# Decoding double-precision weights by way of PSUM in a fused attention and feed-forward kernel

## The chip, the cores and the metric

One core of a Trainium2 chip runs the kernel. The engines are TensorE (PE; its weight loads are listed apart as PEld), VectorE (DVE), ScalarE (ACT), GpSimd (POOL) and the queues that issue transfers (SP here). SBUF is the working memory, PSUM the memory of eight banks into which TensorE writes. The metric is the device time in microseconds of one execution; the median of several runs counts.

## What is computed

Attention over 4 batches, 8 heads, 768 rows and a head size of 64, with a window of 96 rows, 8 global columns and a linear bias; then a feed-forward network (FFN) on the 3072 rows, whose activation is a ratio of two polynomials:

```python
def reference(q, k, v, n_global, n_local, w_in, w_out, a, b):
    scores = q @ k.T / 8 - slope * dist          # kept: local window or global columns
    x = softmax(scores) @ v                      # rows x 512
    h = x @ w_in                                 # 512 -> 2048
    P = a[0] + a[1] * h + a[2] * h**2 + a[3] * h**3
    Q = 1 + abs(b[0]) * abs(h) + abs(b[1]) * h**2
    return (P / (Q + 1e-6)) @ w_out              # 2048 -> 512
```

The weights `w_in` and `w_out` (named `moe_w_in` and `moe_w_out`) arrive as 64-bit floats. [...]

## The kernel before

The rows are worked through in 12 chunks of 256. Attention runs in 96 units (`t` counts them), each a block of 128 rows and two heads; the FFN runs in 96 steps (`f`), eight for each chunk, each with 256 of the 2048 inner columns. Step `f` starts 10 units behind attention at first. In one pass of the loop over `t` stand one attention unit, one FFN step, and for the first 17 units two or four weight pieces to decode (`WSCHED`). A scheduler reorders all of it by the priorities `PRI_A` and `PRI`, and each engine then works through its own list strictly in order.

Names: `tk` are the transposed q and k of a unit, `s` its scores, `pr` its probabilities, `tp` and `pT` these transposed, `o` its output, `x` (later `xh` and `xl`) the FFN's input. `h` is the first product of an FFN step, `fu`, `fa`, `fs` and `q` its activation, `acc` the second product. The first chunk multiplies plain 32-bit weights (`w_..f`, L274 and L353). For the later chunks each weight is split into a high part (`w_..h`, L233) and a low part (`win_l`, `wout_l`, L234), each product made of three (L282 and L358).

A weight piece is 128 rows by 512 columns; there are 32, 16 for each matrix. A transfer of 512 KB brings its words (`r_..`) into one of five buffers, `fetch` starts it. `decode` then makes the piece of the upper word `top` and the lower word `low`: the magnitude of the upper word, scaled by 2^-112 (so that its exponent fits); the top bits of the lower word as an integer (`half` scaled and rounded); sign and that integer joined (L218); and the magnitude shifted by three bits and joined with it (L220). Which engine scales is set for each piece by the table `MODE`: in mode 5 GpSimd scales the magnitude (L211, nine pieces), else ScalarE (L213); `half` is scaled by GpSimd (L215) but for the first piece (L217). Everything of this lies in SBUF. A buffer comes free for the next transfer with the last operation.

PSUM's eight banks are shared out by pools: `ps_h` two (tag h), `ps_o` two (acc), `ps_r` one (tag r, the tile q of the activation), `ps_t` three (tag t: tk, s, tp and o in turn).

Of the kernel before, what the change touches and what calls it, by code (L numbers as in the profile page):

```python
# [9 lines left out]
F32 = mybir.dt.float32  # L10
FR = mybir.dt.float32r
I32 = mybir.dt.int32
BF16 = mybir.dt.bfloat16
U16 = mybir.dt.uint16
AF = mybir.ActivationFunctionType
ALU = mybir.AluOpType
PSUM = bass.MemoryType.PSUM

P = 128
# [3 lines left out]
FLOOR = -0.5 + 2.0 ** -14  # L23
# [16 lines left out]

SPLITS = {4: 0, 5: 2, 6: 4, 7: 8, 8: 12, 9: 16, 10: 19, 11: 22, 12: 25, 13: 28, 14: 32}

MODE = (3, 5, 2, 5, 2, 5, 2, 5, 2, 5, 2, 5, 2, 2, 5, 2, 2, 5, 2, 2, 5, 2, 2, 2, 2, 2, 2, 2, 2, 2, 2, 2)
HI_V = (0, 2, 4, 6, 8, 10, 12, 14, 16, 18, 20, 22, 24, 26, 28, 30)
LO_V = (13, 15, 17, 19, 21, 23, 25, 27, 29, 31)

# [59 lines left out]
def tile_kernel(ctx: ExitStack, tc: tile.TileContext, q, k, v, n_global, n_local,  # L106
                w_in, w_out, ca, cb, out):
    nc = tc.nc
# [5 lines left out]
    TOK = 2 * P  # L114
# [8 lines left out]
    pl = SimpleNamespace(tmps=TMPS, gbufs=GBUFS, split=False)  # L123
# [34 lines left out]
    full = {}  # L158
    hi = {}

    def piece(dt, key):
        return wide.tile([P, 2 * TOK], dt, tag="w", name=f"w{'_'.join(map(str, key))}{'f' if dt is F32 else 'h'}",
                         bufs=NCT * DF // (2 * TOK) + NFT + 1)
# [11 lines left out]
    def fetch(key, eng=nc.sync):  # L175
        z, r, j = (*key, 0)[0:3]
        r = slice(r * P, (r + 1) * P)
        src = w_in_i[r, 4 * j * TOK:4 * (j + 1) * TOK] if z else w_out_i[r, :]
        home = (pl.early, "raw", 2) if (len(full) + len(fetched)) % 5 in (1, 3) else (pl.ffn, "g", pl.gbufs)
        raw = home[0].tile([P, 2, 2, TOK], F32, tag=home[1], name="r" + "_".join(map(str, key)), bufs=home[2])  # L180
        raw = fetched[key] = raw.rearrange("p z a b -> p (z a b)").rearrange("p (f w) -> p f w", w=2)
        eng.dma_start(out=raw.bitcast(I32), in_=src.rearrange("p (f w) -> p f w", w=2))

    def decode(key):
        dst = full[key] = piece(F32, key)
        if key not in fetched:
            fetch(key)
        raw = fetched.pop(key)
        bits = dst.bitcast(I32)
        top, low = raw.bitcast(I32)[:, :, 1], raw.bitcast(I32)[:, :, 0]  # L190
        half = raw.bitcast(U16).rearrange("p f (w z) -> p f w z", z=2)[:, :, 0, 1]
        mode = MODE[len(full) - 1]
        if mode < 2:


            nc.scalar.activation(out=dst, in_=raw[:, :, 1], func=AF.Abs)
            guard = nc.gpsimd if mode else nc.vector
            guard.tensor_scalar(out=dst, in0=dst, scalar1=1.125 * 2.0 ** -15, scalar2=None, op0=ALU.max)
            nc.vector.tensor_scalar(out=bits, in0=bits, scalar1=3, scalar2=0x3FFFFFFF,
                                    op0=ALU.logical_shift_left, op1=ALU.bitwise_and)  # L200
            nc.vector.scalar_tensor_tensor(out=bits, in0=top, scalar=-0x40000000, in1=bits,
                                           op0=ALU.bitwise_and, op1=ALU.bitwise_or)
            nc.vector.scalar_tensor_tensor(out=bits, in0=low, scalar=29, in1=bits,
                                           op0=ALU.logical_shift_right, op1=ALU.bitwise_or)
            return

        if mode == 5:  # L210
            nc.gpsimd.tensor_scalar(out=dst, in0=raw[:, :, 1], scalar1=2.0 ** -112, scalar2=None, op0=ALU.mult)  # L211
        else:
            nc.scalar.activation(out=dst, in_=raw[:, :, 1], func=AF.Abs, scale=2.0 ** -112)  # L213
        if mode != 3:
            nc.gpsimd.tensor_scalar(out=low, in0=half, scalar1=2.0 ** -13, scalar2=FLOOR, op0=ALU.mult, op1=ALU.add)  # L215
        else:
            nc.scalar.activation(out=low, in_=half, func=AF.Copy, scale=2.0 ** -13, bias=FLOOR)  # L217
        nc.vector.scalar_tensor_tensor(out=low, in0=top, scalar=-0x80000000, in1=low,  # L218
                                       op0=ALU.bitwise_and, op1=ALU.bitwise_or)
        nc.vector.scalar_tensor_tensor(out=bits, in0=bits, scalar=3, in1=low,  # L220
                                       op0=ALU.logical_shift_left, op1=ALU.bitwise_or)

    w_in_i = w_in.bitcast(I32)
    w_out_i = w_out.bitcast(I32)
# [333 lines left out]
    def windowed(lates):  # L558
# [33 lines left out]
        for t in range(NU + LAG + F2 + 1):  # L592
# [75 lines left out]
            for n, (kind, j) in enumerate(WSCHED.get(t, ())):  # L668
                tc.cur_priority = base + 1000 * t + pri[False]["dec"] + 50 * n
                for key in pieces(kind, j):  # L670
                    decode(key)
# [162 lines left out]
```

## Time and profile before

| | |
|---|---|
| median of 3 runs | 760.51 us (758.7 to 760.87) |
| the profiled execution | 762.41 us, its span 760.6 us |
| busy in the span | PE 730.6, PEld 635.3, DVE 609.0, ACT 577.6, POOL 455.4 us |
| mean granted clock of TensorE | 0.993 |
| weights decoded | between 8.8 and 100.6 us |
| DVE idle | none between 60 and 97.5 us |
| PE in the chain that ended last | 87% |

The span is cut by what each engine does. Busy time of PE is modelled from its pipelined matmuls, so a PE that waits briefly between two of them still shows as busy; how much it really worked is read from the number of its records and from what one takes where nothing waits. A wait is put down to the event that ended it. Everything that the change touches lies in the first 105 us of the span.

### The profile page before, as it was taken

How to read it: one execution, taken by the hardware profiler on the slowest of the kernel's cores; microseconds unless marked ns; L12 is line 12 of the kernel's file. 1: busy time of each engine (PE TensorE's matmuls, PEld its weight loads, DVE VectorE, ACT ScalarE, POOL GpSimd, SP SyncE). 2: the span in 40 equal slices, each digit the busy share in tenths (PEclk: the TensorE clock that was granted, in tenths of full speed). 3: DMA queues.
4: the chain of work that ended last, by engine and by line, in shares of the span. 5: the costliest groups of instructions: out<-in, count | busy, mean ns of one | idle time of the engine just before them, and what ended most of it. 6: DMA issues, size and time to landing. Idle time of an engine off the chain costs nothing.

```text
span 760.6 us, 15061 instructions
## 1 busy us (share of the span) xinstructions
PE 730.6 (96%) x5072; PEld 635.3 (84%) x5072; DVE 609.0 (80%) x1440; ACT 577.6 (76%) x1302; POOL 455.4 (60%) x488
## 2 busy tenths in 40 slices
PE   4788989999999999999999999999999999999996
PEld 3566657788988988998999989988988988998995
DVE  5789985888798878888788878778888788886565
ACT  5687866986887877877877877877887878776764
POOL 4585665584666666746656656566466656665441
PEclk9999999999999999999999999999999999999999
DMA  8876500204332322323322322233322331200000
GB/s 232 254 245 181 185 22 15 57 22 111 91 79 69 104 64 58 101 64 74 101 53 58 101 61 66 84 78 77 89 59 64 90 72 37 71 16 1 28 1 33
DMA packets 111959, 62.17 MB, mean 82 GB/s; under 512 B 81664, under 2 KB 100096, under 8 KB 111872
## 3 DMA queue, kind: packets, MB, share of 16 engines
q1 hardware_dynamic: 111584, 61.11, 29.8%
q8 instruction: 42, 0.69, 0.4%
q14 instruction: 45, 0.37, 0.2%
q10 hardware_dynamic: 288, 0.00, 0.0%
HBM read 35.92 MB, written 6.29 MB: 55 GB/s over the span
## 4 chain that ended last, share of the span: by engine, by line
PE 87%; DVE 6%; DMA 2%; issue 2%; POOL 1%; ACT 1%; SPq 0%; DVEq 0%; POOLq 0%
PE h L282 34%; PE acc L358 33%; PE o L522 5%; PE tp L497 5%; PE s L449 4%; PE acc L353 3%; DVE r L218 2%; DMA r<-in_moe_w_in_dram 2%; PE s L444 1%; PE tk L394 1%; PE h L274 1%; DMA nat<-in_k_dram 1%; DVE pr L463 1%; PE o L513 0%; POOL r L215 0%
## 5 line engine op out<-in xcount | busy, mean ns | idle before, releaser
L487 POOL TENSOR_SCALAR pr<-pr,stats 128x256 f32<-128x256 f32 (+1 forms) x152 | 132.9, 885 | 108.8 <-DVE stats L478 64.5
L282 PE MATMUL h<-xh,win_l 128*128 128x256 f32 x704 | 197.5, 281 | 0.0
L315 POOL TENSOR_TENSOR fa<-fa,fs 128x512 f32<-128x512 f32 x95 | 125.1, 1317 | 83.2 <-ACT fs L308 73.2
L358 PE MATMUL acc<-wout_l,g 128*128 128x512 f32 x352 | 139.4, 396 | 0.0
L282 PEld LDWEIGHTS h<-xh,win_l 128*128 128x128 f32 x704 | 133.1, 189 | 2.0 <-issue 0.5
L338 POOL TENSOR_TENSOR g<-fu,g 128x512 fp32r<-128x512 f32 x87 | 113.9, 1309 | 32.0 <-ACT g L337 25.9
L473 ACT ACTIVATE pr<-pr,stats 128x256 f32<-128x256 f32 (+1 forms) x192 | 92.7, 485 | 30.8 <-DVE stats L463 28.9
L306 ACT ACTIVATE fu<-h,coef 128x512 f32<-128x512 f32 (+1 forms) x97 | 75.1, 774 | 27.8 <-PE h L282 23.9
L327 DVE SCALAR_TENSOR_TENSOR fu<-fu,coef,q 128x512 f32<-128x512 f32 (+1 forms) x97 | 71.7, 739 | 29.9 <-ACT q L323 27.3
L322 ACT ACTIVATE fs<-fa,coef 128x512 f32<-128x512 f32 (+1 forms) x97 | 69.5, 716 | 27.6 <-POOL fa L315 25.8
L313 DVE TENSOR_TENSOR fu<-fu,h 128x512 f32<-128x512 f32 (+1 forms) x97 | 65.5, 675 | 16.8 <-ACT fs L308 16.7
L358 PEld LDWEIGHTS acc<-wout_l,g 128*128 128x128 f32 x352 | 66.4, 189 | 9.6
L314 DVE SCALAR_TENSOR_TENSOR fu<-fu,coef,h 128x512 f32<-128x512 f32 (+1 forms) x97 | 71.7, 739 | 1.9
L427 DVE SCALAR_TENSOR_TENSOR kq<-tk,kq 64x256 fp32r<-64x256 f32 x144 | 60.8, 422 | 14.7 <-ACT kq L426 10.5
L328 DVE SCALAR_TENSOR_TENSOR q<-fa,coef,q 128x512 f32<-128x512 f32 (+1 forms) x97 | 72.1, 743 | 0.0
L499 DVE COPY pT<-tp 128x512 f32<-128x512 f32 (+1 forms) x75 | 48.4, 645 | 28.0 <-PE tp L497 26.9
L426 ACT ACTIVATE kq<-tk 64x256 fp32r<-64x256 f32 x144 | 54.3, 377 | 19.2 <-DVE kq L427 13.5
L308 ACT ACTIVATE fs<-h,coef 128x512 f32<-128x512 f32 (+1 forms) x97 | 66.3, 684 | 2.0 <-DMA out_dram<-o 1.8
L329 DVE SCALAR_TENSOR_TENSOR fu<-q,fu 128x512 f32<-128x512 f32 (+1 forms) x97 | 66.1, 681 | 1.6
L337 ACT CAST g<-fu 128x512 fp32r<-128x512 f32 (+1 forms) x89 | 54.8, 615 | 15.0 <-DVE fu L329 14.6
L307 ACT ACTIVATE fa<-h,coef 128x512 f32<-128x512 f32 (+1 forms) x97 | 65.6, 676 | 0.0
L497 PE MATMUL tp<-ident,pr 128*128 128x128 f32 x352 | 57.3, 275 | 2.5 <-DVE stats L463 2.4
(253 smaller groups left out, 2049.0 us busy)
## 6 DMA issues: line engine op xcount, KB each, us to landing
mv<-nat SPq DMA_DIRECT2D x36, 256.0 KB
qT<-kq SPq DMA_DIRECT2D x144, 64.0 KB
r<-in_moe_w_in_dram SPq DMA_DIRECT2D x16, 512.0 KB
r<-in_moe_w_out_dram SPq DMA_DIRECT2D x16, 512.0 KB
nat<-in_q_dram SPq DMA_DIRECT2D x48, 128.0 KB
nat<-in_k_dram SPq DMA_DIRECT2D x48, 128.0 KB
vt<-in_v_dram SPq DMA_DIRECT2D x48, 128.0 KB
out_dram<-o SPq DMA_DIRECT2D x24, 256.0 KB
```

The costliest lines, as they stand in the source:

```text
L282: nc.tensor.matmul(out=hps[f][:, y, :], lhsT=w[:, fs], rhs=x[:, ct, :], start=(n == 0), stop=(n == 3 * NCT - 1))
L306: nc.scalar.activation(out=u, in_=h, func=AF.Identity, scale=a3, bias=a2)
L314: nc.vector.scalar_tensor_tensor(out=u, in0=u, scalar=a1, in1=h, op0=ALU.add, op1=ALU.mult)
L315: side(f).tensor_tensor(out=a, in0=a, in1=s, op=ALU.add)
L322: nc.scalar.activation(out=s, in_=a, func=AF.Ln, bias=q1)
L327: nc.vector.scalar_tensor_tensor(out=u, in0=u, scalar=a0, in1=r, op0=ALU.add, op1=ALU.mult)
L328: nc.vector.scalar_tensor_tensor(out=r, in0=a, scalar=q1, in1=r, op0=ALU.add, op1=ALU.mult)
L338: side(f).tensor_tensor(out=g[:, 1, ys], in0=u, in1=g[:, 0, ys], op=ALU.subtract)
L358: nc.tensor.matmul(out=acc, lhsT=gs[f][:, z, y, ts], rhs=w, start=(ft == 0 and n == 0), stop=(ft == NFT - 1 and n == 2))
L473: nc.scalar.activation(out=d, in_=d, func=AF.Exp, scale=-1.0, bias=st[:, x:x + 1], accum_out=st[:, 2 + 2 * x:3 + 2 * x])
L487: nc.gpsimd.tensor_scalar(out=d, in0=d, scalar1=st[:, 6 + x:7 + x], scalar2=None, op0=ALU.mult)
L497: nc.tensor.transpose(out=t_ps[:, x, w, :], in_=pr[:, x, w, :], identity=ident)
```

## The change

The magnitude is no longer made in SBUF: every piece has a tile `mag` in PSUM (name `m`), which ScalarE writes for all 32 pieces. DVE's first operation shifts it and joins it with the scaled lower word, in place in PSUM; the second adds the sign from the upper word and writes the piece to SBUF. GpSimd scales the lower words only, as before (31 of 32). The first 16 pieces take their tile from the pools of h and r, in turn h, r, h; from the 17th on (`IDLE`) they take it from `ps_t`, the attention tiles' pool. No pool gets larger. The branch for modes 0 and 1, which the table did not use, goes too. All lines behind move up by 13.

```diff
-MODE = (3, 5, 2, 5, 2, 5, 2, 5, 2, 5, 2, 5, 2, 2, 5, 2, 2, 5, 2, 2, 5, 2, 2, 2, 2, 2, 2, 2, 2, 2, 2, 2)
+LOW_A = (0,)
+IDLE = 16
...
-        bits = dst.bitcast(I32)
+        n = len(full) - 1
         top, low = raw.bitcast(I32)[:, :, 1], raw.bitcast(I32)[:, :, 0]
         half = raw.bitcast(U16).rearrange("p f (w z) -> p f w z", z=2)[:, :, 0, 1]
-        mode = MODE[len(full) - 1]
...
-        if mode == 5:
-            nc.gpsimd.tensor_scalar(out=dst, in0=raw[:, :, 1], scalar1=2.0 ** -112, scalar2=None, op0=ALU.mult)
+        pool, tag = ((pl.ps_h, "h"), (pl.ps_r, "r"), (pl.ps_h, "h"))[n % 3] if n < IDLE else (pl.ps_t, "t")
+        mag = pool.tile([P, 2 * TOK], F32, tag=tag, name=f"m{n}")
+        bits = mag.bitcast(I32)
+        nc.scalar.activation(out=mag, in_=raw[:, :, 1], func=AF.Abs, scale=2.0 ** -112)
+        if n in LOW_A:
+            nc.scalar.activation(out=low, in_=half, func=AF.Copy, scale=2.0 ** -13, bias=FLOOR)
         else:
-            nc.scalar.activation(out=dst, in_=raw[:, :, 1], func=AF.Abs, scale=2.0 ** -112)
-        if mode != 3:
             nc.gpsimd.tensor_scalar(out=low, in0=half, scalar1=2.0 ** -13, scalar2=FLOOR, op0=ALU.mult, op1=ALU.add)
-        else:
-            nc.scalar.activation(out=low, in_=half, func=AF.Copy, scale=2.0 ** -13, bias=FLOOR)
-        nc.vector.scalar_tensor_tensor(out=low, in0=top, scalar=-0x80000000, in1=low,
-                                       op0=ALU.bitwise_and, op1=ALU.bitwise_or)
         nc.vector.scalar_tensor_tensor(out=bits, in0=bits, scalar=3, in1=low,
                                        op0=ALU.logical_shift_left, op1=ALU.bitwise_or)
+        nc.vector.scalar_tensor_tensor(out=dst.bitcast(I32), in0=top, scalar=-0x80000000, in1=bits,
+                                       op0=ALU.bitwise_and, op1=ALU.bitwise_or)
```

In the new program the scaling is L200 (ACT) and L204 (POOL), DVE's two operations are L205 and L207; h is made in L261, acc in L340, the scores in L431.

The scheduler's order changes with it. First place: PE, where the FFN begins (step 0 is h_567 before and h_583 after; s_497 is the score of unit 8, s_572 that of unit 9). Before:

```order
L444 MATMUL s_497<-kF,qz 128x256 x2
L400 MATMUL tk_508<-ident,nat_284 128x128 x2
L274 MATMUL h_567<-x_269,w_0_0f 128x256
L274 MATMUL h_567<-x_269,w_1_0f 128x256
L274 MATMUL h_623<-x_269,w_0_0f 128x256
L274 MATMUL h_623<-x_269,w_1_0f 128x256
L497 MATMUL tp_514<-ident,pr_463 128x128 x4
```

After:

```order
L431 MATMUL s_572<-kF,qz 128x256 x2
L387 MATMUL tk_588<-ident,nat_365 128x128 x2
L509 MATMUL o_535<-pT_533,vt_218 64x128 x2
L509 MATMUL o_535<-pT_533,vt_115 64x128 x2
L484 MATMUL tp_607<-ident,pr_515 128x128 x4
L261 MATMUL h_583<-x_273,w_0_0f 128x256
L261 MATMUL h_583<-x_273,w_1_0f 128x256
```

The early matmuls of steps 0 and 1, which used the first half of x, are gone; the FFN starts one unit later in the list, with x complete. Before, PE goes on with step 0 behind the score of unit 10.

Second place: DVE, where x for the first chunk becomes complete (x_269 before, x_273 after) and the first activation follows. Before:

```order
L218 SCALAR_TENSOR_TENSOR r_2_2_484<-r_2_2_484 128x512
L220 SCALAR_TENSOR_TENSOR w_3_2f<-w_3_2f,r_3_2_491 128x512
L220 SCALAR_TENSOR_TENSOR w_2_2f<-w_2_2f,r_2_2_484 128x512
L544 TENSOR_TENSOR x_269<-x_269,o_521 128x2x128
L463 ISA pr_616,stats<-s_612,masks 128x256
```

After:

```order
L207 SCALAR_TENSOR_TENSOR w_2_2f<-r_2_2_496,m_498 128x512
L531 TENSOR_TENSOR x_273<-x_273,o_535 128x2x128
L463 TENSOR_REDUCE stats<-stats 128x2
L465 RECIPROCAL stats<-stats 128x2
L205 SCALAR_TENSOR_TENSOR m_506<-m_506,r_3_2_504 128x512
L207 SCALAR_TENSOR_TENSOR w_3_2f<-r_3_2_504,m_506 128x512
L205 SCALAR_TENSOR_TENSOR m_554<-m_554,r_0_2_552 128x512
L207 SCALAR_TENSOR_TENSOR w_0_2f<-r_0_2_552,m_554 128x512
L205 SCALAR_TENSOR_TENSOR m_562<-m_562,r_1_2_560 128x512
```

The piece w_3_2f stands behind x now. m_554 (the 15th piece) is the last but one magnitude in a bank of h, so step 0's h_583 can have that bank only behind L207 for w_0_2f, four decode operations after x.

Third place: DVE in the stretch where magnitudes lie in the attention tiles' banks. After:

```order
L205 SCALAR_TENSOR_TENSOR m_1040<-m_1040,r_12_1038 128x512
L316 SCALAR_TENSOR_TENSOR fu_1093<-q_1160,fu_1093 128x512
L465 RECIPROCAL stats<-stats 128x2
L205 SCALAR_TENSOR_TENSOR m_1048<-m_1048,r_13_1046 128x512
L207 SCALAR_TENSOR_TENSOR w_12f<-r_12_1038,m_1040 128x512
L207 SCALAR_TENSOR_TENSOR w_13f<-r_13_1046,m_1048 128x512
```

Two magnitudes are held at once, two of the three banks of `ps_t`; L316 of step 6 (fu_1093) stands ahead of the pieces of w_out for that step. Before, w_12f was decoded ahead of the activation of step 3:

```order
L218 SCALAR_TENSOR_TENSOR r_11_932<-r_11_932 128x512
L220 SCALAR_TENSOR_TENSOR w_10f<-w_10f,r_10_925 128x512
L314 SCALAR_TENSOR_TENSOR fu_811<-fu_811,coef,h_793 128x512
L233 CAST w_2_0h<-w_2_0f 128x512
L220 SCALAR_TENSOR_TENSOR w_12f<-w_12f,r_12_1010 128x512
L218 SCALAR_TENSOR_TENSOR r_13_1017<-r_13_1017 128x512
```

So decoding is spread over more FFN steps, the activations of all eight steps of the first chunk now stand ahead of the last decoded piece on DVE (of five steps before, the fifth in part), and the splitting of weights follows behind it.

More of the change, by code (lines that the diff above doesn't have):

```diff
@@ L188, in decode @@
         raw = fetched.pop(key)
-        bits = dst.bitcast(I32)
+        n = len(full) - 1
         top, low = raw.bitcast(I32)[:, :, 1], raw.bitcast(I32)[:, :, 0]
         half = raw.bitcast(U16).rearrange("p f (w z) -> p f w z", z=2)[:, :, 0, 1]
-        mode = MODE[len(full) - 1]
[L193 to L201, printed above, removed]
-                                           op0=ALU.bitwise_and, op1=ALU.bitwise_or)
-            nc.vector.scalar_tensor_tensor(out=bits, in0=low, scalar=29, in1=bits,
-                                           op0=ALU.logical_shift_right, op1=ALU.bitwise_or)
-            return
@@ L215, in decode @@
+        if n in LOW_A:
+            nc.scalar.activation(out=low, in_=half, func=AF.Copy, scale=2.0 ** -13, bias=FLOOR)
+        else:
             nc.gpsimd.tensor_scalar(out=low, in0=half, scalar1=2.0 ** -13, scalar2=FLOOR, op0=ALU.mult, op1=ALU.add)
-        else:
-            nc.scalar.activation(out=low, in_=half, func=AF.Copy, scale=2.0 ** -13, bias=FLOOR)
-        nc.vector.scalar_tensor_tensor(out=low, in0=top, scalar=-0x80000000, in1=low,
-                                       op0=ALU.bitwise_and, op1=ALU.bitwise_or)
```

## The prediction

> **What bounds the kernel now.** I read the chain of waits first, to see which engine sets the end, and from when on.
>
> ```profile
> PE 87%; DVE 6%; DMA 2%; issue 2%; POOL 1%; ACT 1%; SPq 0%; DVEq 0%; POOLq 0%
> ...
> 96.85 0.61 DVE fu L329
> ...
> 97.51 5.40 PE acc L353 x8
> ...
> 103.34 3.46 PE h L274 x16
> 106.80 0.86 PE s L444 x4
> ...
> 119.29 0.47 PE o L513 x5
> ...
> 119.87 0.87 PE o L522 x15
> 120.74 5.35 PE acc L353 x12
> 126.09 0.44 PE tp L497 x4
> ...
> 130.94 0.22 PE tk L400 x2
> ...
> 743.31 10.50 PE acc L358 x44
> ```
>
> TensorE (PE) is 87% of the chain. From 97.5 us to the last matmul at 753.8 the chain holds nothing but PE: there the time is the sum of its work, which the change leaves alone. So only PE's idle time before 97.5 us can be won or lost, apart from new waits behind it. The rows in the middle also price PE's work when it is not waiting: L274 takes 3.46/16 = 216 ns a record, L353 446, L444 215, L497 and L400 110, L513 94, L522 58. Right behind its wait L353 took 5.40/8 = 675 ns, so the eight lost (675 - 446) x 8 = 1.8 us more, at a lower granted clock (below).
>
> Next, the busy time of each engine by stretch (columns: PE, PE's weight loads, DVE = VectorE, ACT = ScalarE, POOL = GpSimd, then granted clock, DMA share, GB/s).
>
> ```profile
> 20.00:30.00 10.00, 7.04 (x39) 4.73 (x38) 6.88 (x23) 6.59 (x27) 3.19 (x5) 0.83 0.89 269
> 30.00:47.20 17.20, 13.42 (x101) 10.13 (x101) 15.35 (x43) 12.99 (x41) 14.19 (x16) 1.00 0.78 245
> 47.20:60.00 12.80, 10.58 (x67) 8.68 (x68) 11.24 (x23) 10.11 (x25) 11.98 (x12) 1.00 0.78 249
> 60.00:97.50 37.50, 33.11 (x170) 23.10 (x168) 37.50 (x71) 28.43 (x65) 21.29 (x22) 1.00 0.54 165
> 97.50:130.00 32.50, 32.49 (x146) 21.64 (x147) 23.82 (x59) 21.07 (x50) 19.92 (x20) 0.95 0.06 13
> ```
>
> From 60 to 97.5 us DVE has no idle moment, and from 30 to 60 POOL is busy 26.2 of 30 us. These are the two engines that the change relieves. The DMA engines are at 0.54 to 0.89: no bound by themselves.
>
> I cut at 47.2 us, where PE takes up the FFN matmuls for good (stage A before, stage B from there to 97.5). PE's busy time counts waiting inside a matmul, so I take records from the trace, in stage B, for L274, L353, L444, L497, L522, L400 and L513 in this order:
>
> ```profile
> 47.20:97.50 50.30, 20.43 (x88) 16.21 (x88) 1.00 0.60 187
> 47.20:97.50 50.30, 11.00 (x24) 4.32 (x24) 1.00 0.60 187
> 47.20:97.50 50.30, 5.34 (x20) 3.56 (x20) 1.00 0.60 187
> 47.20:97.50 50.30, 3.06 (x20) 2.39 (x20) 1.00 0.60 187
> 47.20:97.50 50.30, 3.57 (x48) 2.68 (x48) 1.00 0.60 187
> 47.20:97.50 50.30, 2.29 (x12) 1.70 (x12) 1.00 0.60 187
> 47.20:97.50 50.30, 2.19 (x24) 1.23 (x24) 1.00 0.60 187
> ```
>
> Times the prices above: 88 x 0.216 + 24 x 0.446 + 20 x 0.215 + 20 x 0.110 + 48 x 0.058 + 12 x 0.110 + 24 x 0.094 = 42.6 us of work in 50.3. PE truly idles only 7.7 us in stage B, and with the 1.8 us behind it 9.5 us. That is all that stage B can give back, however much faster decoding gets.
>
> **The change, part by part.** First DVE: the same 64 decode operations, but each reads one input from PSUM.
>
> ```profile
> L218 DVE SCALAR_TENSOR_TENSOR r<-r x32: 674/693/1753, 10.8 to 96.2; 128x512 int32<-128x512 int32 x32
> 0.00:47.20 47.20, 10.42 (x14) 0.96 0.83 246
> 47.20:97.50 50.30, 16.11 (x18) 1.00 0.60 187
> 0.00:47.20 47.20, 10.91 (x14) 0.96 0.83 246
> 47.20:97.50 50.30, 15.53 (x17) 1.00 0.60 187
> L313 DVE TENSOR_TENSOR fu<-fu,h 128x512 f32<-128x512 f32 x6 | 4.0, 675 | 0.0
> L314 DVE SCALAR_TENSOR_TENSOR fu<-fu,coef,h 128x512 f32<-128x512 f32 x6 | 4.4, 734 | 0.0
> L329 DVE SCALAR_TENSOR_TENSOR fu<-q,fu 128x512 f32<-128x512 f32 x5 | 3.4, 677 | 0.0
> ```
>
> The first row gives shortest, median and longest: 674, 693 and 1753 ns, so some run 2.6 times as long as others of one shape. The next four are L218 and L220 by stage. At 0.68 us each, stage A's 28 would take 19.0 us and took 21.3: 2.3 us of stretching. Stage B's 35 would take 23.8 and took 31.6: 7.8 us. In the same stretch the operations with one input in PSUM (h, and q in L329) are not stretched at all, 675 to 734 ns on average; L314 has a per-partition scalar, which the decode has not. I read the stretching as GpSimd standing in the way of operations with two SBUF inputs, and price the new ones at 0.68 us, like L329, which has a constant scalar and one PSUM input: DVE gains 2.3 us in A and 7.8 in B. Bounds: 0.67 (L313) to 0.73 (L314), which would take back 64 x 0.05 = 3.2 us of the 10.1.
>
> [...]
>
> Second, GpSimd loses its nine scalings (L211), and ScalarE takes them.
>
> ```profile
> sum 130.00, POOL 15.47; mean POOL 5.16
> L213 ACT ACTIVATE w_2f<-r x4: 654/664/688, 39.1 to 48.6; 128x512 f32<-128x512 f32 x4
> L323 ACT ACTIVATE q<-fs 128x512 f32<-128x512 f32 x6 | 3.6, 604 | 2.6 <-DVE fu L329 2.6
> DVE r L218 <- POOL r L215: 1.5, 3, 0.8
> ```
>
> L211 is 15.5 us of POOL, in the stretch where POOL was nearly full. On the path it is worth what DVE waited for POOL's L215 between 20 and 47 us: 1.5 us. ScalarE gets nine at 0.66 us, 5.9 us, less what writing PSUM saves on all 32 (L323, PSUM out, 0.60): about 4 us in all. It had 50.3 - 38.5 = 11.8 us free in stage B and 4.2 of 17.2 between 30 and 47: I cost it at nothing. If that cover were gone it would be 4 us.
>
> Third, the PSUM banks. Sixteen decodes use the banks of h and q before the FFN needs them, sixteen (from w_4f on) those of the attention tiles. The order shows two consequences.
>
> ```profile
> PE h L274 <- DVE x L544: 0.6, 1, 0.6
> 0.00:47.20 47.20, 1.91 (x9) 1.47 (x9) 0.96 0.83 246
> PE h L274 <- DVE fu L314: 2.2, 1, 2.2
> PE acc L353 <- DVE fu L329: 2.0, 1, 2.0
> L463 DVE CUSTOM_DVE_ANT_0 pr<-s,masks 128x256 f32<-128x256 f32 x24 | 9.1, 414 | 1.1 <-PE s L444 1.1
> ```
>
> (a) Stage A. Before, PE had 1.9 us of L274 done ahead of 47.2 and then waited only for x. Now h gets its bank when w_0_2f is decoded, and DVE has four decode operations between x and that: 4 x 0.68 = 2.7 us later. PE also has one score (0.86 us) less done by then. Against it: x comes 2.3 (stretching) + 1.5 (POOL) + 1.4 (two decode operations that the order put behind x) = 5.2 us sooner. Sum: 5.2 - 2.7 - 1.9 - 0.9 = -0.3 us, so nothing; between -4 and +4, since x also hangs on attention's own round trips.
>
> (b) Stage B. One FFN step with one attention unit is 16 x 0.216 + 8 x 0.446 + 2.4 (4 L444, 4 L497, 2 L400, 4 L513, 8 L522) = 9.4 us of PE. DVE's part of a step is five FFN operations at 0.68 to 0.73, 3.5 us; attention, two score passes at 0.41 and, by estimate, as much again in small operations, 1.7; and 14 decodes over eight steps, 1.75 at 1.36 us, 2.4: 7.6 us, where stretching (7.8 us in the stage) and weight casts had filled it up. So PE becomes the longest engine, with some start-up: waits like the two above for fu, 2.2 and 2.0 us, remain in kind, and decode tiles now hold up to two of three attention banks (the order has two of them in flight). I leave 5 us of the 9.5 as waits, between 2 and 9.5: gain 4.5.
>
> (c) Behind stage B all weight splitting comes later in the order, next to its use; I cost this at nothing to 3 us, taking 0.
>
> Sum: 0 + 4.5 - 0 = 4.5 us. The profiled execution took 762.41 us (span 760.6), 1.9 over the median of 760.51; taken off the median: **756 us**.
>
> **Rivals.**
>
> - *Decoding is the bound and all of it comes back.* For it: DVE without idle in the row 60:97.50. Against it: PE's 42.6 us of work in 50.3. It needs both stages: 9.5 + 2 from A, 749 us.
> - *No change.* Stage A loses what stage B wins (A at -4), or the dearer PSUM price holds (3.2 us of DVE): 758.5 to 762 us.
> - *Slower: the attention banks.* PE works in order. Where a transpose or score waits for a bank that a decode tile holds, every FFN matmul behind it waits too. One tile is held for the ACT write and two DVE operations, 0.66 + 2 x 0.68 = 2.0 us. Eight pairs of decodes come in that stretch; if each pair stops PE 2.0 us, 16 us go against 9.5, so 767 us. It decides from 9.5/8 = 1.2 us a pair. Against it: bank holders come from engines that then have room, and PE has FFN work ahead of most of these.
>
> **How the numbers follow.** I tell no change within 0.3% (2.3 us) of the median. Chances: my forecast 0.48, all of it back 0.13 (faster together 0.61); no change 0.21; slower by the banks 0.18. The forecast's own range is 751 to 758 (gain 2.3 to 9.5). Over all cases 747 to 765 leaves out about 2 in 10: beyond 749 for a better stage A, and most but not all of the bank case.
>
> **What would show it.** L205 and L207 all at 0.67 to 0.73 us, none above 1 us. POOL under 7 of 10 us between 30 and 60. First L261 matmul (FFN) later in PE's order, at 43 to 48 us, and then one stretch without holes. The chain going over to PE alone earlier than 97.5. Wrong if PE waits for m tiles, or for ACT behind POOL, in sum over 9.5 us after the FFN starts, or if x comes no sooner than 46 us.

## The result: slower, 772.57 us, and the profile after

The changed kernel takes 772.57 us in the median of five runs (771.55 to 773.49), the kernel before 760.51 (five runs, 757.45 to 763.45). The ratio is 1.0161, with a 95% interval of 1.0128 to 1.0195: 12 us slower, where 4.5 us faster was forecast. The profiled executions took 771.55 us (span 769.8) and 762.41 us (span 760.6).

First the same stretches of the kernel after, with two later ones, and behind them these two of the kernel before (columns as in the prediction: PE, PEld, DVE, ACT, POOL, granted clock, DMA share, GB/s).

```profile
20.00:30.00 10.00, 7.88 (x43) 5.23 (x40) 5.76 (x23) 6.66 (x25) 2.33 (x5) 1.00 0.84 268
30.00:47.20 17.20, 11.90 (x92) 8.09 (x90) 15.41 (x50) 16.01 (x48) 5.68 (x12) 1.00 0.84 259
47.20:60.00 12.80, 11.42 (x44) 9.60 (x45) 7.49 (x14) 5.20 (x11) 5.79 (x9) 0.74 0.73 255
60.00:97.50 37.50, 37.50 (x180) 25.77 (x179) 30.91 (x64) 28.35 (x62) 12.09 (x16) 1.00 0.45 133
97.50:130.00 32.50, 29.71 (x152) 19.36 (x150) 22.10 (x55) 21.72 (x57) 12.89 (x16) 1.00 0.15 37
130.00:160.00 30.00, 28.93 (x225) 25.58 (x225) 21.28 (x56) 28.30 (x72) 21.69 (x20) 1.00 0.19 51
160.00:220.00 60.00, 55.91 (x378) 47.39 (x378) 53.10 (x128) 45.99 (x107) 43.43 (x45) 1.00 0.33 84
```

```profile
130.00:160.00 30.00, 30.00 (x213) 24.70 (x213) 24.21 (x51) 26.56 (x62) 20.15 (x17) 1.00 0.17 46
160.00:220.00 60.00, 60.00 (x428) 53.31 (x427) 50.61 (x125) 48.95 (x112) 37.01 (x41) 1.00 0.33 85
```

Between 60 and 97.5 us all that was hoped for has come: PE is busy throughout, DVE has 6.6 us idle where it had none, POOL two thirds of the time. The loss is on both sides of it. Ahead of it, PE is busy for 11.90 of the 17.2 us between 30 and 47 us (13.42 before), and the granted clock in the 12.8 us behind this is 0.74 on average. Behind it, where the kernel before is busy without a gap, PE lacks 2.8 us between 97.5 and 130 us, 1.1 between 130 and 160 and 4.1 between 160 and 220, with 378 records done there in place of 428. The chain says the same: its shares by engine, and pieces of it in order of time (start and duration in us).

```profile
PE 85%; ACT 6%; DVE 5%; DMA 2%; issue 1%; SPq 0%; DVEq 0%; ACTq 0%
```

```profile
111.54 0.90 PE o L509 x16
112.45 0.69 DVE w_13f L207
113.14 0.86 DVE w_0h L220
...
119.74 0.53 ACT pT L486
...
135.13 0.78 ACT fu L293
...
152.66 0.62 ACT fs L309
...
181.70 0.78 DVE win_l L221
183.70 2.06 DMA qT<-kq
185.90 0.59 PE s L436 x3
...
199.61 0.68 DVE wout_l L221
202.18 0.75 DVE q L315
204.09 2.08 DMA qT<-kq
206.30 0.59 PE s L436 x3
```

Before, only PE stood in the chain from 97.5 us. Now, from 112 to 206 us, DVE has 35 us of it, ACT 35 and PE 18, and behind that it is PE's again; weight casts (`w_0h`, L220) and subtractions (`win_l`, `wout_l`, L221) are among them.

Busy time of PE hides short waits, so I count its work: records of each PE line by the prediction's prices, 0.110 us for L269, L381 and 0.220 for L345, L436 (with these, 300 to 500 us comes to 200.3 us of work before and 200.4 after). By that count the kernel after stands 4.4 us behind the kernel before at 60 us, 2.9 ahead at 110, 9.1 behind at 220, and 8.7 behind at 740 us; the spans differ by 9.2. So there are three terms: **-4.4, +7.3, -12.0**. The experiments are read with this count. Two cautions. A record that lies across the edge of a window is counted on both sides; counted once, the terms are -3.8, +7.0 and -11.7, and single figures of the table below move by up to 0.9 us. And the profiled execution of before was some 3 us slower than its median in the comparisons below (759.0 to 759.7), so a kernel 3 us ahead in this count only equals it in the median.

### The profile page after: what moved, and what is told of

Same layout as the page of the kernel before. It is cut to its first block, busy times and chain, and to the rows that moved or that the text cites. A ratio compares the mean times of both kernels' runs of the same rounds, so it can differ in the third digit from the quotient of the medians.

```text
span 769.8 us, 15078 instructions
## 1 busy us (share of the span) xinstructions
PE 735.3 (96%) x5072; PEld 638.2 (83%) x5072; DVE 599.9 (78%) x1440; ACT 581.2 (76%) x1311; POOL 429.7 (56%) x479
## 4 chain that ended last, share of the span: by engine, by line
PE 85%; ACT 6%; DVE 5%; DMA 2%; issue 1%; SPq 0%; DVEq 0%; ACTq 0%
PE h L269 30%; PE acc L345 30%; PE o L509 5%; PE s L436 4%; PE tp L484 4%; PE h L261 4%; PE acc L340 3%; PE s L431 2%; ACT pr L460 1%; PE tk L381 1%; DMA nat<-in_k_dram 1%; ACT fu L293 1%; PE o L500 1%; PE tk L387 1%; ACT qz L400 1%
## 5 line engine op out<-in xcount | busy, mean ns | idle before, releaser
L269 PE MATMUL h<-xh,win_l 128*128 128x256 f32 x704 | 197.2, 281 | 1.4 <-DVE win_l L221 0.8
L302 POOL TENSOR_TENSOR fa<-fa,fs 128x512 f32<-128x512 f32 x95 | 123.2, 1296 | 90.4 <-ACT fs L295 84.0
L345 PE MATMUL acc<-wout_l,g 128*128 128x512 f32 x352 | 139.2, 397 | 0.8 <-DVE wout_l L221 0.8
L269 PEld LDWEIGHTS h<-xh,win_l 128*128 128x128 f32 x704 | 132.8, 189 | 3.9 <-DVE win_l L221 1.0
L345 PEld LDWEIGHTS acc<-wout_l,g 128*128 128x128 f32 x352 | 66.3, 188 | 10.8 <-DVE wout_l L221 1.2
L316 DVE SCALAR_TENSOR_TENSOR fu<-q,fu 128x512 f32<-128x512 f32 (+1 forms) x97 | 66.0, 681 | 1.6
```

The source lines that it names most:

```text
L269: nc.tensor.matmul(out=hps[f][:, y, :], lhsT=w[:, fs], rhs=x[:, ct, :], start=(n == 0), stop=(n == 3 * NCT - 1))
L302: side(f).tensor_tensor(out=a, in0=a, in1=s, op=ALU.add)
L345: nc.tensor.matmul(out=acc, lhsT=gs[f][:, z, y, ts], rhs=w, start=(ft == 0 and n == 0), stop=(ft == NFT - 1 and n == 2))
```

## Experiments

| kernel | first split, us | work against before at 48 / 110 / 220 us | median, us | ratio to before, 95% |
|---|---|---|---|---|
| after | 112.2 | -3.6 / +2.9 / -9.1 | 772.57 | 1.0128 to 1.0195 |
| e1: pieces 1 to 16 in PSUM | 80.7 | +0.3 / +1.3 / -0.4 | 765.66 | 1.0057 to 1.0112 |
| e2: pieces 17 to 32 in PSUM | 115.0 | -1.8 / +0.4 / -10.6 | 773.58 | 1.0153 to 1.0205 |
| e3: none in PSUM, ScalarE scales all | 79.4 | +0.7 / +1.6 / +0.3 | 763.46 | 1.0032 to 1.0069 |
| e4: pieces 1 to 12 in PSUM | 81.1 | +2.6 / +2.4 / +2.1 | 761.92 | 1.0019 to 1.0052 |
| h2: after, eight splits sooner | 89.8 | -3.0 / +5.2 / +0.3 | 765.67 | 1.0058 to 1.0111 |
| f2: all in banks of h and q | 98.3 | +0.5 / +7.8 / +2.2 | 764.75 | 1.0047 to 1.0101 |
| f3: pieces 1 to 24 in PSUM | 88.7 | -3.6 / -0.3 / -2.2 | 764.34 | 1.0044 to 1.0101 |
| f5: e4, GpSimd scales three again | 82.8 | +2.6 / +2.8 / +1.1 | 766.30 | 1.0069 to 1.0123 |
| g1: f2, eight splits sooner | 83.5 | -0.6 / +6.0 / +3.5 | 759.90 | 1.0003 to 1.0022 |
| g3: f2, all splits sooner | 83.2 | -0.5 / +6.5 / +4.3 | 760.54 | 1.0003 to 1.0022 |
| g4: before, eight splits sooner | 75.9 | +1.1 / -3.8 / -3.8 | 765.09 | 1.0067 to 1.0105 |
| k1: g1, pieces 13 to 16 in acc's banks | 77.8 | +1.0 / +5.8 / +6.0 | 758.42 | 0.9971 to 0.9991 |

The first split of the kernel before starts at 84.8 us.

**Which half of the pieces (e1, e2).** In e1 pieces 17 to 32 go through SBUF with the old two operations; in e2 (`range(16, 32)`) the other half does, and GpSimd scales seven of it as before. The lines that choose:

```diff
+IN_PSUM = range(0, 16)
...
+        if n in IN_PSUM:
...
+            mag = pool.tile([P, 2 * TOK], F32, tag=tag, name=f"m{n}")
+        else:
+            mag = dst
```

> Pieces 1 to 16 by way of PSUM as in the changed kernel, pieces 17 to 32 in SBUF (ScalarE scales all, GpSimd none). Theory 1 (the attention tiles' banks): from the 17th piece on, magnitudes take two of attention's three banks, so attention falls some three units behind the first chunk's FFN, and it and the weight splitting are made up for between 110 and 220 us, where TensorE then lacks work: 12 us lost there. This kernel should lose at most 3 us behind 110 us, keep the lost 4 us of the FFN's late start, and lose the 7 us won between 60 and 110 us in part: 761 to 766 us, first weight split before 95 us. Rival 2 (ScalarE has all the scaling, and GpSimd's missing operations change the order): nothing of that is undone here, so 769 us or more, first split behind 105 us.

> The other half: pieces 1 to 16 as before the change (in SBUF, with GpSimd scaling seven of them), pieces 17 to 32 in the attention tiles' banks (ScalarE scales). Theory 1: the FFN starts by 47.5 us, the gain of some 6 us between 60 and 110 us is kept, and the loss of 12 us behind 110 us stays whole: 765 to 769 us, first split behind 105 us. Rival 2: GpSimd scales seven of nine again, so within 3 us of the kernel before: 758 to 763 us.

The late loss goes with the second half: from 110 to 220 us e1 loses 1.7 us, e2 11.0. e2 is as slow as the whole change, although GpSimd scales seven pieces in it; its time is 4.6 us above the range that I expected, since the gain between 60 and 110 us is only 2 us in it. e1's time lies in its range, but not by the sum that I gave: the early 4 us are not lost in it, and the later gain is lost whole. Rival 2 (ScalarE's share) falls: in e1 ScalarE has all of it. What ties splitting to decoding is seen in the starts of the first split and of the 30th piece (w_13f). In before and in e1 ScalarE writes that piece first, in after and e2 DVE's second operation does, since the magnitude lies elsewhere:

```profile
L213 ACT ACTIVATE w_13f<-r x1: 679/679/679, 84.2 to 84.2; 128x512 f32<-128x512 f32 x1
L233 ACT CAST w_0h<-w_0f x2: 603/609/615, 84.8 to 98.1; 128x512 fp32r<-128x512 f32 x2
```

```profile
L207 DVE SCALAR_TENSOR_TENSOR w_13f<-r,m x1: 690/690/690, 112.4 to 112.4; 128x512 int32<-128x512 int32 x1
L220 ACT CAST w_0h<-w_0f x2: 607/616/624, 112.2 to 123.5; 128x512 fp32r<-128x512 f32 x2
```

The first fence is before, the second after (shortest, median, longest in ns; first and last start). In e1 the two start at 80.2 and 80.7 us, in e2 at 115.2 and 115.0, in e3 78.8 and 79.4, in f3 88.7 and 88.7, in f2 97.9 and 98.3. Whole pieces and their high parts take turns in one set of 33 buffers, and in the program the first split stands behind pieces 29 and 30. So the scheduler puts it where they are first written: it starts within 0.6 us of that in these seven kernels and in e4, 1.9 us behind it in f5. It waits for no signal there: in the kernel after, ACT is busy up to the split's start, and only the split's place in its list has moved. h2 below shows it from the other side: there the first splits stand ahead of these pieces in the program, and the first starts at 89.8 us, though piece 30 is written at 111.3. (Lowering the priority numbers of the splits by 3000 instead moves no instruction in any engine's list.)

**The scaling alone (e3).** `IN_PSUM` is empty and ScalarE scales all.

> The kernel before with only the scaling moved: ScalarE scales all 32 magnitudes, in SBUF, GpSimd none; no magnitude in PSUM. Theory 1: no bank is taken, GpSimd is 15 us freer, ScalarE has 6 us more: 757 to 762 us, first split before 95 us. Rival 2: most of the loss is here already, 768 us or more. It also shows whether decode operations with two SBUF inputs still stretch (median by stage 0.7 to 1.1 us before) when GpSimd scales none: if GpSimd's scaling is what stretches them, the longest falls under 1.3 us and the stage from 60 to 97 us has DVE idle time.

Little late loss (1.3 us from 110 to 220 us), but 4 us slower than before in the median, a little over theory 1's range. The stretching question is answered against both signs that I named: DVE is still busy for 37.44 us of the 37.5 from 60 to 97.5 us, and the longest operation is still far over 1.3 us; from 47.2 to 105 us the 36 decode operations took 0.85 us on average (14.15 + 16.33 us in all) against 0.93 before (16.11 + 17.28), the longest 1748 ns. So GpSimd's scaling was at most a part of what stretches them.

**The banks of h (e4).** As e1 with `range(0, 12)`.

> Pieces 1 to 12 by way of PSUM (banks of h and q), pieces 13 to 32 in SBUF, ScalarE scales all. It differs from the kernel with 16 pieces in PSUM by pieces 13 to 16 alone, which hold the two banks of h until the FFN's first step. Theory 1: the FFN starts by 46 us and not at 48.6, so 3 to 5 us faster than that kernel, 757 to 761 us. Rival 3 (the FFN's start hangs on x and attention's round trips, the banks only came last by chance): within 1.5 us of it.

3.7 us faster than e1, as theory 1 says (the time itself is 0.9 us over its range), and 2.3 us more PE work by 48 us: its early FFN matmuls start at 38.0 us again, e1's first at 48.7. But the bank of h is the smaller part of the early loss. e1 and the kernel after start the FFN at the same time and stand 3.9 us apart in work by then. PE's rows of both from 42.5 us, after first:

```profile
42.57 0.38 PE L387 MATMUL tk<-ident,nat 128*128 128x128 f32 x2
42.88 0.66 PE L509 MATMUL o<-pT,vt 128*64 128x128 f32 x8
43.88 0.66 PE L484 MATMUL tp<-ident,pr 128*128 128x128 f32 x4 [0.34 <-ACT kF L402]
48.58 3.78 PE L261 MATMUL h<-x,w_0f 128*128 128x256 f32 x8 [4.05 <-DVE w_2f L207]
...
57.33 1.03 PE L431 MATMUL s<-kF,qz 128*128 128x256 f32 x4
```

```profile
43.25 1.10 PE L441 MATMUL s<-kF,qz 128*128 128x256 f32 x4
44.19 0.38 PE L397 MATMUL tk<-ident,nat 128*128 128x128 f32 x2
45.04 0.66 PE L494 MATMUL tp<-ident,pr 128*128 128x128 f32 x4 [0.47 <-ACT pT L496]
45.63 0.66 PE L510 MATMUL o<-ident,stats 128*64 128x128 f32 x8
...
46.65 1.13 PE L441 MATMUL s<-kF,qz 128*128 128x256 f32 x4
...
48.74 3.50 PE L271 MATMUL h<-x,w_0f 128*128 128x256 f32 x15
```

e1 fills the wait with two more attention units. After the change the next score takes its bank behind the magnitudes of pieces 17 and 18, which ScalarE writes at 48.3 and 50.4 us; in PE's list it stands behind 28 matmuls of h, and starts at 57.3 us. So PE stands for 4 us. f3 and f2 below bear this out: with these two magnitudes in attention's banks the early loss is there (-3.6 us at 48 us), without them it is not (+0.5).

**Splits sooner (h2).** The kernel after with one table changed:

```diff
-SPLITS = {4: 0, 5: 2, 6: 4, 7: 8, 8: 12, 9: 16, ...}
+SPLITS = {2: 0, 3: 2, 4: 4, 5: 8, 6: 8, 7: 8, 8: 12, 9: 16, ...}
```

> The changed kernel, with the splitting of the first eight weight pieces written two units sooner in the program (the other splits where they were). In the changed kernel the first split starts at 112 us, in the same microsecond in which the 29th and 30th decoded pieces are written, because all pieces share one rotation of buffers. Theory 1a (the late splits are what TensorE lacks between 110 and 220 us): first split at 95 to 105 us and half or more of the 12 us lost there comes back, 762 to 767 us. Theory 1b (the lag of attention's own units is the larger part, splits only add to it): within 3 us of the changed kernel, 769 to 774 us.

Theory 1a: 6.9 of the 12 us come back (5.8 by the two ratios, each against before in its own comparison), and the magnitudes still lie in attention's banks. PE is 93% of the chain, where it was 85%. From 110 to 220 us 4.9 us are lost in place of 12.0.

**Other banks, and half a dose (f2, f3).** `IDLE = 32` (f2); `range(0, 24)` in e1's edit (f3).

> The changed kernel, with the magnitudes of pieces 17 to 32 too in the banks of h and q (in turn h, q, h), none in the attention tiles' banks. Everything else, ScalarE's scaling and both DVE operations with an input in PSUM, stays. Theory 1 (attention's three banks are the matter): the first split starts before 95 us, behind 110 us no more than 3 us are lost, and the FFN steps of the first chunk pay a little for shared banks: 760 to 767 us. Rival 4 (any bank that decoding takes while the FFN runs costs as much): 770 us or more, with TensorE waiting in the first chunk's FFN.

> A half dose: pieces 1 to 16 in the banks of h and q, 17 to 24 in the attention tiles' banks, 25 to 32 in SBUF (ScalarE scales all). Theory 1a (late splits): the 29th and 30th piece no longer wait for a bank, the first split is as early as with 16 pieces in PSUM (81 us) or little later, so 764 to 767 us. Theory 1b (attention's lag): half of the way from 765.7 (16 pieces in PSUM) to 772.6 us (all), 768 to 771 us.

In f2 all operations of the change stay, only attention's banks are free: the early loss is gone, PE is 7.8 us ahead at 110 us, and rival 4 falls. Its time lies in theory 1's range, but it gives 5.6 us back by 220 us, where at most 3 were expected, its first split being at 98.3 us and not before 95. In f3 the first split comes at 88.7 and the loss from 110 to 220 us is 1.9 us: not half of the whole change's, but what theory 1a says. It keeps the early loss whole (-3.6 at 48 us), as pieces 17 and 18 are in attention's banks.

**GpSimd's three scalings (f5).** e4 with `BY_POOL = (14, 17, 20)`.

> Pieces 1 to 12 by way of PSUM, 13 to 32 in SBUF as before the change, GpSimd scaling the magnitudes of pieces 15, 18 and 21 as it did. It keeps the start of the FFN (some 3 us sooner than before by 48 us) and gives the three scalings back to GpSimd. ScalarE scaling all 32 in SBUF was 4 us slower than before; if that is the price of moving the scaling where DVE and ScalarE are full, this kernel is 3 us faster than with ScalarE scaling all (761.9): 756 to 760 us. If ScalarE's share is not the reason, 760 to 764 us.

A miss: 4.4 us slower than e4, not faster, and slower than both ranges. This speaks against ScalarE's share as the reason why e3 and e4 are slower than before; what the reason is stays open. The four kernels that decode late pieces in SBUF with a new order lie between 762 and 766 us.

**Both edits, and a control (g1, g3, g4).** g1 is f2 with h2's table; g3 has all splits sooner (`{2: 0, 3: 4, 4: 8, 5: 10, 6: 13, ...}`); g4 is the kernel before with h2's table.

> All 32 magnitudes in the banks of h and q, none in attention's, and the splitting of the first eight pieces written two units sooner. With all magnitudes in the banks of h and q, TensorE had done 8 us more work by 140 us than the kernel before, and gave 6 of it back between 160 and 220 us, with the first split at 98 us. Theory 1a (late splits are what it gives back): most of the 6 us stays, 756 to 760 us, no slower than the kernel before (759.0). Rival 5 (the 6 us are DVE's and ScalarE's work put off, which has to be done in any case; it only moves): 762 to 765 us, as without the edit.

> The same with all splits written one to two units sooner and at an even pace (3 in each step instead of 4). Theory 1a: as with the first eight sooner or up to 2 us better, 755 to 760 us. Rival 5: 762 us or more.

> The control: the kernel before the change, with the splitting of its first eight pieces written two units sooner. Its splits start at 85 us already, and behind 97.5 us TensorE alone sets its end, so theory 1a expects no gain, 758 to 761 us. If sooner splits are worth 7 us to any order of this kernel, 752 to 754 us.

g1 is 4.9 us faster than f2, and 0.1% slower than before: the late splits were the larger part of what f2 gave back (g1 gives back 2.5 us of work from 110 to 220 us, f2 5.6), and rival 5 falls. g3 adds nothing to it. The control goes the other way, 6 us slower than before, which neither expectation had. Sooner splits are thus no gain in themselves. Before, DVE has no idle moment from 60 to 97.5 us, and g4 loses 4.9 us of work between 48 and 110: I read this as the splits pushing decoding and the FFN back there. They gained only in the kernels in which decoding by way of PSUM had made room.

**One more bank (k1).** g1, and pieces 13 to 16 in the banks of acc:

```diff
+        pool, tag = (pl.ps_o, "acc") if 12 <= n < 16 else ((pl.ps_h, "h"), (pl.ps_r, "r"), (pl.ps_h, "h"))[n % 3]
```

> The kernel with all magnitudes outside attention's banks and the first eight splits sooner, with one more change: pieces 13 to 16 take the two banks of acc, which are empty until the first chunk's second product, in place of h's. Pieces 13 to 16 in h's banks were worth 2.3 us of TensorE's work by 48 us (12 against 16 pieces in PSUM). If that comes through to the end, 757 to 758.5 us, faster than the kernel before (759.1); if attention fills that time in any case, 759 to 761 us, the same as without this edit.

758.42 us, against 759.70 of before in the same comparison: a ratio of 0.9981 (0.9971 to 0.9991), so faster than the kernel before, if by 1.3 us only, and by far than the kernel after. From 60 to 220 us PE has no gap in it:

```profile
60.00:97.50 37.50, 37.50 (x178) 25.45 (x175) 33.88 (x75) 29.51 (x69) 17.73 (x24) 1.00 0.50 154
97.50:130.00 32.50, 32.50 (x163) 22.29 (x160) 22.80 (x46) 23.83 (x51) 18.23 (x17) 1.00 0.10 21
130.00:160.00 30.00, 30.00 (x220) 26.02 (x219) 25.15 (x58) 25.30 (x61) 21.71 (x19) 1.00 0.13 37
160.00:220.00 60.00, 60.00 (x430) 53.35 (x428) 50.96 (x124) 48.59 (x109) 38.59 (x42) 1.00 0.33 86
```

## Why the prediction was wrong

**The price of a decode operation: right.** 0.68 us was forecast, none above 1 us:

```profile
L205 DVE SCALAR_TENSOR_TENSOR m<-m,r x32: 676/698/715, 10.7 to 119.8; 128x512 int32<-128x512 int32 x32
```

The longest operation of L207 takes 690 ns. Shortest and median of L205, with one input in PSUM, are 676 and 698 ns, against 674 and 693 for L218, whose inputs lay in SBUF. POOL was freed as forecast, too (11.5 of 30 us busy between 30 and 60, where under 7 in ten had been said).

**(b) Stage B: right in kind, too small.** 4.5 us were forecast, and 7.3 came between 60 and 110 us (6.4 counted from 48). PE's 42.6 us of work in 50.3 was the right reading; fewer waits were left than the 5 us I kept.

**(a) Stage A: wrong.** I had 0 (-4 to +4), and it lost 4.4 by 60 us. x was complete at 45.3 us in place of 47.1, so 1.8 us sooner and not 5.2. The wait for h's bank was seen (w_0_2f ended at 48.5, 3.2 us behind x; forecast 2.7). What the sum left out is that PE has nothing else to do meanwhile, because attention's next score stands behind two magnitudes in its banks, and that the clock falls (0.74 granted on average from 47.2 to 60 us): the first 28 records of L261 took 8.90 us, 318 ns each against 216.

**(c) Weight splitting: the step that failed.** It was costed at nothing to 3 us and entered as 0, without a working; from 110 to 220 us 12.0 us were lost, by itself enough to turn +4.5 into a loss. I saw in the order that splitting came later, but did not sum up how much work that put off. Splitting is 64 operations of DVE, ACT and POOL. Before, they ran from 84.8 to 175.9 us and began beside the first chunk's FFN; now they ran from 112.2 to 207.6 us. So they began when the last h of that chunk was done (107.1 us), and fell together with the second chunk's FFN and with attention, which was two units behind (60 records of its score by 110 us, against 68). The first matmul of the second chunk's FFN came at 125.0 us in place of 116.4 (118.7 in h2). From 112 to 206 us DVE and ACT set the pace: 69 of 94 us of the chain, POOL none.

How much of the 12.0 us is the splits' is read from h2, which moves them alone: 7.1 us of them go. The other 4.9 are in part the banks': g1, which differs from h2 in the banks only, loses 2.5 us there. For these 2.5 us no run gives a cause.

**The rivals.** The bank rival (0.18) had the right cause and the right side, but not the place, and its 767 us were too few: I let PE stop by 2.0 us at each of eight pairs of decodes while the first chunk's FFN ran. From 60 to 97.5 us it did not stop at all, since it had FFN work ahead. The lag was handed on, through the buffers shared by whole and split pieces, to a stretch that I had called closed ("from 97.5 us the chain holds nothing but PE"). That chain described the order of before; it does not say how much slack the other engines have there. The chain was to go over to PE alone sooner than at 97.5 us, and did so at 206. Nor does everything that the change touches lie in the first 105 us, as the part on the time before has it: the splits that it moved ran up to 207.6 us.

## What to carry to other kernels

When an edit moves the first write of a tile from one operation to a later one, look for everything that takes its buffer behind it in the program: here a cast that needed nothing of the new operations was put 27 us later in its engine's list. Where one engine is the whole chain in a stretch, that can be so because the others have done their work ahead; sum up what the edit puts off into that stretch, not only what it makes faster. And in this kernel scratch tiles cost least in the banks of stages that had them to spare (h and q, and acc while it is empty), most in those of the stage that has to run ahead.

## What the runs showed of the hardware that was not expected

Operations of DVE with both inputs in SBUF are stretched also when GpSimd scales no magnitude: 666 to 1748 ns in e3. Those with one input in PSUM were not, 715 ns at most in 64 in the kernel after. The trace of before has what ran on GpSimd during each of its 64 (L218, L220): the 21 that took 878 ns or more had 0.37 us or more of GpSimd's operations beside them, 17 of the 21 none of its scaling (L211); the 12 with nothing beside them took 670 to 696 ns. In the kernel after, 14 of the 64 had 0.37 us or more beside them and took 700 ns at most. Such overlap is not all of the cause, as 23 more in before had as much and took 674 to 723 ns. So GpSimd's lower words and its other work may explain what I had put down to its scaling alone; no run takes these away to show it.

PE's wait costs twice in the kernel after. PE stands from 44.5 to 48.6 us, and from 47.0 to 53.9 us the granted clock is 0.50 (columns: PE, granted clock, DMA share, GB/s):

```profile
46.50:47.00 0.50, 0.00 (x0) 1.00 1.08 322
47.00:47.50 0.50, 0.00 (x0) 0.54 1.36 309
...
53.50:54.00 0.50, 0.50 (x3) 0.63 0.92 336
54.00:54.50 0.50, 0.50 (x4) 1.00 0.97 393
```

The clock fell 2.5 us into the wait. In the kernel before it fell to 0.50 at 23.2 and 98.3 us, behind waits of 1.7 and 2.4 us, each time for 3.4 us, while waits of 2.2 and 2.0 us at 56 and 74 us left it at 1.00. So the length of a wait alone does not tell in these traces whether the clock falls. In e1, where attention filled the time, no such drop stands in the rows from 20 to 80 us (1.00 each).
